# Log sums of a gated scan as two float32r products of a split operand, with a new table of priorities

## The chip, the cores and the metric

The kernel runs on one core of a Trainium2 chip. The metric is the device time of one execution in microseconds (us), as the median of several runs. A profile is one further execution, recorded by the hardware profiler.

## The reference

A complex gated linear attention (4 batches, 8 heads, 768 steps, head size 48) is followed by a token mixer of low rank and a channel mixer with a hidden size of 1536.

```python
mag = np.sqrt(a_re * a_re + a_im * a_im)
scale = np.minimum(mag, 0.999) / (mag + 1e-06)
a_re_n, a_im_n = (a_re * scale, a_im * scale)
for t in range(S):
    ar, ai = (a_re_n[:, :, t, :, None], a_im_n[:, :, t, :, None])
    new_re = ar * S_re - ai * S_im
    new_im = ar * S_im + ai * S_re
    kv = np.einsum('bhd,bhe->bhde', k[:, :, t], v[:, :, t])
    S_re, S_im = (new_re + kv, new_im)
    y[:, :, t] = np.einsum('bhd,bhde->bhe', q[:, :, t], S_re)
...
x = y.transpose(0, 2, 1, 3).reshape(B, S, H * D)      # (4, 768, 384)
h = x.transpose(0, 2, 1) @ U @ V                      # rank 32 over the tokens
u = x + h.transpose(0, 2, 1)
out = u + np.maximum(u @ w_ch1, 0.0) @ w_ch2
```

## The kernel before

**Chunks and groups.** The 4 x 768 tokens are cut into 24 chunks of 128 tokens (`i`, six to a batch), and the chunks into 12 groups of two (`g`). A gate is worked as a log magnitude and an angle, a group at a time. `gates(g)` returns four stages, recorded one after the other: `magnitudes` (L561), `totals` (L623), `turns` (L654) and `waves` (L698). Group 0 is worked chunk by chunk, all others in operations over 128 x 768 elements, two chunks of 384.

**The log sums.** `magnitudes_of` makes `l` (the tile `GL`, one buffer), which is minus the log of the clipped magnitude; the last step, an addition on VectorE, is L594 (L591 in group 0). For each of the two chunks `within` (L607) then has TensorE multiply `l` by two constant 128 x 128 matrices, `mid` and `fore`, which GpSimd makes at the start from a triangular matrix of zeros and ones, `prefix`, as differences of its columns; they hold -1, 0 and 1. The first product gives each token's log sum to the middle of its block of eight tokens (`es ps`), the second that from the block middles to the end of the half chunk (`ef ps`). Both are made in float32 at L611. ScalarE takes exponentials of them: `es` weighs q and k (`weigh`, L729), `ef` weighs k for the state (`onto_end`, L751). `of_blocks` (L637) makes 28 further sums of each column of `l` (`tot`, 16 small products a chunk, L647); they become the table `T` of decays between blocks. In the plan, `tot` comes behind the sums of its group through the name `("sums", g)`.

**The chunk.** `prep(i)` turns q and k by the angles and transposes them on TensorE (`tr`, L745) into the tile `QK`. `chain(i)` makes the products within blocks (`inner`, L784), scales `QK` between them on VectorE (`times`, L794, whose work the profile shows at L331), makes the `corners` (L830), the state's update (`dk`, L855) and the output (`y`, L886 and L894) into `xo`.

**The mixer.** `mixer(m)` works two chunks. When the six chunks of a batch are there, their rank-32 products (`mixed`, L928, copied to `r`) are made; then come a second `mixed` product per pair (L944), its addition to `xo` (L334), a transposition (`uTp`, L957), the products with w_ch1 (`up`, L969; in the last five mixers `few`, L1027) and those with w_ch2 (`down`, L1115 and L1158). The weights come in as pieces that ScalarE or VectorE and then three VectorE operations (L509 to L511) decode.

**The order.** The kernel doesn't issue its instructions where they stand in the source. Each operation is recorded by `PE`, `ACT`, `DVE`, `POOL` or `SP` (L303 to L316) with an engine, a cost, a rank, what it reads and what it writes. `Plan.order` (L80) then runs through time with these costs and gives each free engine the ready operation of the lowest priority value; this fixes one order for each engine, and the chip's engines work theirs strictly in that order. The priorities come from the table `URGENCY` (L26) by kind of work (`gates`, `angles`, `prep`, `levels`, `rest`, `w1`, `w2`) and number of the chunk or piece, and from `urgency` (L255) for the rest. As long as no mixer has begun and TensorE has nothing ready, the plan puts in a product of the identity with itself (`spare`, L1288), which nobody reads.

Of the kernel before, what the change touches and what calls it, by code (L numbers as in the profile page):

```python
# [9 lines left out]

FP = mybir.dt.float32
I32 = mybir.dt.int32
U32 = mybir.dt.uint32
AF = mybir.ActivationFunctionType
OP = mybir.AluOpType
PSUM = bass.MemoryType.PSUM

CH = 128
# [4 lines left out]
GC = 2  # L23
BLK = 32

URGENCY = {  # L26
    "w1": {0: 68.6, 1: 298.27, 2: 3233.01, 3: -108.72, 4: -43.26, 5: 87.5, 6: 342.55},
    "w2": {0: 1285.36, 2: 1292.54, 4: -1719.29, 6: -645.54, 8: 615.72, 10: -28.39, 12: 295.27},
    "gates": {0: -839.53, 1: -629.56, 2: -1280.45, 4: -490.35, 6: -36.77, 8: 432.19, 10: 283.33, 12: 174.0,
        14: -427.91, 16: -1044.12, 18: 390.39, 20: 16.15, 22: 442.09},  # L30
    "angles": {0: 244.5, 1: 803.69, 2: -1267.4, 4: -662.84, 6: 346.13, 8: -381.86, 10: -1492.55, 12: 857.33,
        14: 238.92, 16: -1275.26, 18: 27.58, 20: -452.39, 22: 700.28},
    "prep": {0: 403.21, 1: -1122.66, 2: -716.65, 3: -727.95, 4: -1687.67, 5: -1146.33, 6: -1196.73, 7: 372.34,
        8: -1231.6, 9: -737.98, 10: -968.71, 11: -301.11, 12: -1415.74, 13: -596.98, 14: 796.35, 15: -1516.54,
        16: 396.83, 17: 113.38, 18: 726.77, 19: -2850.56, 20: 477.2, 21: -682.71, 22: -1187.86, 23: -124.41},
    "levels": {0: -753.29, 1: -1075.23, 2: -3433.49, 3: -627.65, 4: -1402.65, 5: -2863.57, 6: 632.01, 7: 254.71,
        8: 403.03, 9: 467.1, 10: 379.45, 11: -2734.42, 12: -967.09, 13: 651.03, 14: -1988.63, 15: -5.33,
        16: -1244.43, 17: -678.34, 18: -1272.19, 19: 439.17, 20: -494.89, 21: -1132.39, 22: 188.76, 23: -7.55},
    "rest": {0: 430.24, 1: -1218.14, 2: -304.77, 3: -320.19, 4: 73.38, 5: 237.11, 6: 799.33, 7: 863.71, 8: 367.2,
        9: -579.61, 10: -1264.07, 11: -364.98, 12: -1258.34, 13: -1713.0, 14: -1491.2, 15: -35.56, 16: -1243.36,  # L40
        17: 71.85, 18: 200.85, 19: -580.61, 20: 849.69, 21: 576.05, 22: -124.73, 23: -299.46},
}


# [144 lines left out]
def kernel(  # L189
# [24 lines left out]
    nc = tc.nc  # L214
# [3 lines left out]
    DM = H * D  # L218
# [20 lines left out]
    NG = len(GROUPS)  # L239

    PAIRED = 5

    EARLY, SPREAD = 3, (0,)

    TA, TC, TQ, TK, TF, TH, NTOT = 0, 8, 12, 16, 18, 26, 28
    NP = 128 // R
# [7 lines left out]
    singles = pool("singles")  # L254
# [20 lines left out]
    def ring(base, tag, tiles):  # L275

        plan.buffer(base, tag, len(tiles))
        n = plan.turn[base] % len(tiles)
        makers[base] = lambda: tiles[n]

    def get(*base):
        if base not in T:
            T[base] = makers[base]()
        return T[base]
# [8 lines left out]
    def c_dve(n):  # L293
        return 0.15 + 0.00104 * n

    def c_one(n):
        return 0.15 + 0.00052 * n
# [5 lines left out]
    def PE(*a, **kw):  # L303
        plan.add("PE", *a, late=0.17, **kw)
# [4 lines left out]
    def DVE(cost, *a, **kw):  # L309
        plan.add("DVE", cost - 0.09, *a, late=0.09, **kw)  # L310
# [9 lines left out]
    def table(cost, rank, f, reads=(), writes=()):  # L320

        ACT(cost, rank, f, reads=list(reads) + [TABLE], writes=writes)
# [4 lines left out]
    def act(o, i, f, **kw):  # L327
        return nc.scalar.activation(out=o, in_=i, func=f, **kw)  # L328
# [21 lines left out]

    prefix = singles.tile([128, CH], FP, name="prefix")
    mask = singles.tile([128, 6, BLK], I32, name="mask")
    mid = singles.tile([128, CH], FP, name="mid")
    fore = singles.tile([128, CH], FP, name="fore")
    total = singles.tile([128, NTOT], FP, name="total")
    nc.gpsimd.memset(total, 0.0)
    F = singles.tile([128, GC, DM], FP, name="F")
    w1 = singles.tile([128, KD, FF], FP, name="w1")
    w2 = singles.tile([128, KF, DM], FP, name="w2")
# [26 lines left out]
    make_identity(nc, ident)  # L386

    GL = [singles.tile([128, GC * DM], FP, name="GL")]

    tail = ident[:, 127:128].to_broadcast([128, CH])  # L390
    AT, DG, VP = [], [], []
# [86 lines left out]
    def single(p, rank, to, o, pieces):  # L478
# [17 lines left out]
        x = lambda: get("cx", p)[:, 0:n]  # L496
        b, word = o.bitcast(U32), lambda a: a.bitcast(I32)
        one, two = c_one(n), c_dve(n)
# [45 lines left out]
    def gates(g):  # L544


        x, y, l, n, ar, ai = [(nm, g) for nm in ("x", "y", "l", "n", "ar", "ai")]
        z = y
        first = GROUPS[g][0]
        on_dve = g in SPREAD  # L550

        def of(b, i):
            return get(*b)[:, (i - first) * DM:(i - first + 1) * DM]
# [12 lines left out]
        def magnitudes_of(lo, hi):  # L566
            t, R1, W = t_of(lo, hi), ("gates", lo), (hi - lo) * DM
            ca, cd = c_act(W), c_dve(W)
            X, L, N = (b + (lo,) for b in (x, l, n))
            Y = [y + (i,) for i in range(lo, hi)]  # L570
            AR, AI = ([b + (i,) for i in range(lo, hi)] for b in (ar, ai))
            ACT(ca, R1, lambda: act(t(x), t(ar), AF.Square), AR, [X])
            ACT(ca, R1, lambda: act(t(y), t(ai), AF.Square), AI, Y)
            DVE(cd, R1, lambda: add(t(x), t(x), t(y)), Y, [X])
            DVE(c_one(W), R1, lambda: nc.vector.tensor_scalar(out=t(x), in0=t(x), scalar1=M2LO, scalar2=M2HI, op0=OP.max,
                                                              op1=OP.min), [], [X])
            if on_dve:
                DVE(c_one(W), R1, lambda: nc.vector.tensor_scalar(out=t(n).bitcast(U32), in0=t(ar).bitcast(U32), scalar1=0x7FFFFFFF, scalar2=None,
                                                                  op0=OP.bitwise_and), AR, [N])
            else:  # L580
                ACT(ca, R1, lambda: act(t(n), t(ar), AF.Abs), AR, [N])
            table(ca, R1, lambda: act(t(l), t(x), AF.Ln), [X], [L])
            table(ca, R1, lambda: act(t(x), t(l), AF.Exp, scale=0.5), [L], [X])
            DVE(cd, R1, lambda: add(t(x), t(x), t(n)), [N], [X])
            table(ca + 0.09, R1, lambda: act(t(y), t(l), AF.Exp, scale=-0.5, bias=leps), [L], Y)
            table(ca, R1, lambda: act(t(y), t(y), AF.Ln, bias=1.0), [], Y)

            if on_dve:
                DVE(c_one(W), R1, lambda: nc.vector.tensor_scalar(out=t(l), in0=t(l), scalar1=-0.5, scalar2=-LNMAX, op0=OP.mult,
                                                                  op1=OP.max), [], [L])  # L590
                DVE(cd, R1, lambda: add(t(l), t(l), t(y)), Y, [L])  # L591
            else:
                ACT(ca + 0.09, R1, lambda: act(t(l), t(l), AF.Relu, scale=-0.5, bias=lmax), [], [L])
                DVE(cd, R1, lambda: nc.vector.scalar_tensor_tensor(out=t(l), in0=t(l), scalar=LNMAX, in1=t(y), op0=OP.subtract,  # L594
                                                                   op1=OP.add), Y, [L])
            table(ca, R1, lambda: act(t(x), t(x), AF.Ln), [], [X])
            table(ca, R1, lambda: act(t(x), t(x), AF.Exp, scale=-1.0), [], [X])
            DVE(cd, R1, lambda: mul(t(x), t(x), t(ai)), AI, [X])
            if on_dve:
                DVE(c_one(W), R1, lambda: nc.vector.tensor_scalar(out=t(n), in0=t(ar), scalar1=0.0, scalar2=0.5, op0=OP.is_ge,  # L600
                                                                  op1=OP.subtract), AR, [N])
            else:
                ACT(ca + 0.09, R1, lambda: act(t(n), t(ar), AF.Sign, bias=tiny), AR, [N])
            for i in range(lo, hi):
                within(i, R1, L)

        def within(i, R1, L):  # L607
            ps, es = ("es ps", i), ("es", i)

            def summed(m, name, to, keeps):  # L610
                PE(0.65, R1, lambda: nc.tensor.matmul(out=get(*to), lhsT=m, rhs=of(l, i), start=True, stop=True),  # L611
                   [L, name], [to, ("sums", g, i)], takes=[keeps], steps=2)
            psum(ps, "T", [128, DM], [128, 512])
            buffer(es, "es", 3, [128, 2, DM])
            summed(mid, ("mid", 0), ps, es)
            for u in range(2):
                table(c_act(DM), R1, lambda u=u: act(get(*es)[:, u], get(*ps), AF.Exp, scale=1.0 - 2 * u), [ps], [es + (u,)])
            pf, ef = ("ef ps", i), ("ef", i)
            psum(pf, "T", [128, DM], [128, 512])
            summed(fore, ("fore", 0), pf, ef)  # L620
            table(c_act(DM), R1, lambda: act(get(*ef), get(*pf), AF.Exp, scale=-1.0), [pf], [ef])
# [722 lines left out]
```

## Time and profile before

| | |
|---|---|
| median of 3 runs | 688.33 us (687.19 to 691.46) |
| the profiled execution: its own time | 688.27 us |
| its span, first to last instruction | 686.5 us |
| granted TensorE clock, mean | 0.997 |
| TensorE products busy | 664.0 us (97%) |
| VectorE busy | 495.9 us (72%) |
| ScalarE busy | 413.8 us (60%) |

In the lines of the profile PE is a product on TensorE, PEld the load of its weights, DVE is VectorE, ACT is ScalarE, POOL is GpSimd and SP the engine that issues most transfers. A line of a group gives the source line, the engine, the operation, output<-inputs, the shapes and the count, then the busy time and the mean duration in ns, then the engine's idle time just before and what ended it. A product's duration holds its way through the array, so that products overlap; what one costs is seen from the distance of their starts, as the chain in order of time gives it (start, duration, what). A "pass" is one product instruction in the profile.

### The profile page before, as it was taken

The page shows a single profiled execution, that of the slowest core. Times are in us where ns is not written, and L with a number is a line of the kernel's source. Part 1 is how long each engine was busy: PE and PEld are TensorE (multiplying, and loading weights), DVE is VectorE, ACT ScalarE, POOL GpSimd, SP SyncE. Part 2 cuts the span into 40 slices and gives each one's busy share as a digit, 9 for nine tenths or more (in the row PEclk, how much of TensorE's full clock was granted, in tenths as well). Part 3 has the DMA queues.
Part 4 walks back from the last instruction along what each step waited for, and adds up shares of the span by engine and source line. Part 5 has one row for each costly group of instructions (what it writes and reads, how often), then busy time and mean ns, then how long its engine had stood idle before and what let it go on. Part 6 is the DMA issues. An engine that isn't in the chain of part 4 may idle for free.

```text
span 686.5 us, 26452 instructions
## 1 busy us (share of the span) xinstructions
PE 664.0 (97%) x11854; PEld 576.5 (84%) x11854; DVE 495.9 (72%) x882; ACT 413.8 (60%) x791; POOL 40.9 (6%) x81
## 2 busy tenths in 40 slices
PE   8999998999999999999999999999999989999998
PEld 7877776776888888788888888798899988999998
DVE  6798999657878867657685785396996855564734
ACT  6699999687596875937847767457435215031230
POOL 6000000001000000010010000000010000000000
PEclk9999999999999999999999999999999999999999
DMA  7756455461242330610514242112201001000000
GB/s 193 192 96 158 91 126 96 142 183 45 45 94 58 87 68 10 119 43 11 118 44 77 49 89 44 33 49 40 59 23 33 7 21 18 24 1 24 7 18 24
DMA packets 163329, 45.64 MB, mean 66 GB/s; under 512 B 158416, under 2 KB 160016, under 8 KB 163216
## 3 DMA queue, kind: packets, MB, share of 16 engines
q1 hardware_dynamic: 161008, 39.60, 26.7%
q0 software_dynamic: 2208, 4.35, 1.8%
q8 instruction: 93, 1.52, 0.9%
q14 instruction: 20, 0.16, 0.1%
HBM read 33.59 MB, written 4.72 MB: 56 GB/s over the span
## 4 chain that ended last, share of the span: by engine, by line
PE 78%; DVE 8%; ACT 6%; issue 2%; DVEq 0%; ACTq 0%
PE down L1158 18%; PE up L969 15%; PE few L1027 10%; PE inner L784 6%; PE tr L745 4%; PE dk L855 3%; PE y L894 3%; PE es ps L611 2%; PE down L1115 2%; PE ph L689 2%; PE ef ps L611 2%; PE spare L1288 2%; ACT gate L328 2%; PE y L886 2%; PE tot L647 1%
## 5 line engine op out<-in xcount | busy, mean ns | idle before, releaser
L969 PE MATMUL up<-uT,w 128*128 128x256 f32 x504 | 116.1, 382 | 0.0
L969 PEld LDWEIGHTS up<-uT,w 128*128 128x128 f32 x504 | 94.0, 190 | 15.2 <-DVE uT L959 0.3
L331 DVE TENSOR_TENSOR QK<-QK,T 112x512 f32<-112x512 f32 (+1 forms) x144 | 99.8, 715 | 7.4 <-PE corners L830 4.7
L748 ACT COPY QK<-tr 112x512 f32<-112x512 f32 x96 | 52.4, 586 | 43.3 <-PE tr L745 43.0
L328 ACT ACTIVATE gate<-gate 128x768 f32<-128x768 f32 (+1 forms) x89 | 69.3, 793 | 9.7 <-PE ph L689 6.8
L1158 PE MATMUL down<-w,h 128*128 128x192 f32 x396 | 73.5, 330 | 1.2 <-ACT gate L328 1.2
L1158 PEld LDWEIGHTS down<-w,h 128*128 128x128 f32 x396 | 64.1, 190 | 4.7 <-ACT gate L328 1.5
L1035 ACT COPY h<-few 128x512 f32<-128x512 f32 x30 | 17.4, 584 | 70.6 <-PE few L1027 62.5
L784 PEld LDWEIGHTS inner<-QK 112*32 112x32 f32 x4608 | 45.1, 109 | 17.3 <-issue 13.1
L745 PE MATMUL tr<-ident,QKC 128*112 128x128 f32 x384 | 52.9, 276 | 3.8 <-ACT QK L748 2.0
L334 DVE TENSOR_TENSOR h<-few,h 128x512 f32<-128x512 f32 x45 | 31.1, 692 | 34.3 <-PE few L1027 30.4
L784 PE MATMUL inner<-QK 112*32 112x16 f32 (+1 forms) x4608 | 50.7, 190 | 4.2 <-issue 3.9
L331 DVE TENSOR_TENSOR QKC<-qk,cs 128x768 f32<-128x768 f32 x48 | 45.0, 953 | 9.2 <-issue 3.4
L745 PEld LDWEIGHTS tr<-ident,QKC 128*112 128x112 f32 x384 | 42.2, 134 | 10.5 <-ACT QK L748 3.3
L1288 PE MATMUL spare<-ident 128*128 128x128 f32 x336 | 48.2, 291 | 1.9 <-POOL ident masks.py:199 1.4
L1288 PEld LDWEIGHTS spare<-ident 128*128 128x128 f32 x336 | 43.5, 201 | 5.7 <-issue 1.5
L334 DVE TENSOR_TENSOR xo<-down,xo 128x192 f32<-128x192 f32 (+1 forms) x79 | 29.7, 386 | 23.7 <-PE down L1158 23.5
L328 ACT ACTIVATE h<-up 128x512 f32<-128x512 f32 x42 | 24.9, 592 | 33.2 <-PE up L969 33.0
L1158 PE MATMUL down<-stage 128*128 128x192 f32 x198 | 36.8, 327 | 0.7 <-issue 0.7
L1027 PE MATMUL few<-gate,w 128*128 128x128 f32 x280 | 37.2, 282 | 0.0
L903 ACT COPY xo<-y 64x192 f32<-64x192 f32 x96 | 30.0, 313 | 8.7 <-PE y L894 7.0
L790 DVE COPY_PREDICATED DG<-mask,inner 128x128 f32<-128x128 int32 (+1 forms) x72 | 24.5, 343 | 14.6 <-PE inner L784 14.5
(137 smaller groups left out, 1217.7 us busy)
## 6 DMA issues: line engine op xcount, KB each, us to landing
stage<-in_moe_w_ch_dram SPq DMA_DIRECT2D x12, 768.0 KB, 5.2
gate<-in_a_re_dram SPq DMA_DIRECT2D x24, 192.0 KB, 3.5
gate<-in_a_im_dram SPq DMA_DIRECT2D x24, 192.0 KB, 4.0
qk<-in_q_dram SPq DMA_DIRECT2D x24, 192.0 KB, 2.9
qk<-in_k_dram SPq DMA_DIRECT2D x24, 192.0 KB, 3.4
VP<-in_v_dram SPq DMA_DIRECT2D x24, 192.0 KB, 3.7
AT<-DG SPq DMA_DIRECT2D x96, 32.0 KB, 2.0
out_dram<-xo POOLq DMA_DIRECT2D x12, 192.0 KB, 2.3
```

The source lines that it names most:

```text
L328: return nc.scalar.activation(out=o, in_=i, func=f, **kw)
L331: nc.vector.tensor_tensor(out=o, in0=a, in1=b, op=OP.mult)
L334: nc.vector.tensor_tensor(out=o, in0=a, in1=b, op=OP.add)
L611: PE(0.65, R1, lambda: nc.tensor.matmul(out=get(*to), lhsT=m, rhs=of(l, i), start=True, stop=True), [L, name], [to, ("sums", g, i)], takes ...
L745: nc.tensor.transpose(out=get(*ps)[0:DQ, j], in_=get(*qkc)[:, hh * HH + j].rearrange("p u d -> p (u d)")[:, 0:DQ], identity=ident)
L748: ACT(c_act(HH * CH) - 0.05, R1, lambda u=u, hh=hh, ps=ps: nc.scalar.copy(out=get(*QK)[:, u, hh * HH:(hh + 1) * HH], in_=get(*ps)[0:DQ]), ...
L784: nc.tensor.matmul(out=get(*ps)[js, h], lhsT=k_of(h)[:, js], rhs=part(q_of(h)[:, js], "p"), start=True, stop=True, tile_position=(0, j * BLK))
L903: ACT(c_act(HH * D) - 0.06, RR, lambda r=r, u=u: nc.scalar.copy(out=get(*xi).rearrange("p (a u d) -> p a u d", u=2, d=D)[r * HC:(r + 1) * ...
L969: nc.tensor.matmul(out=get(*ps)[:, e], lhsT=w1[:, f, (ff + e) * 128:(ff + e + 1) * 128], rhs=get(*uT)[:, f], start=(f == 0), stop=(f == KD ...
L1027: nc.tensor.matmul(out=get(*ps)[:, q], lhsT=w()[:, q * 128:(q + 1) * 128], rhs=v[0](), start=(n == 0 and q == 0), stop=True, skip_group_ch ...
L1158: nc.tensor.matmul(out=get(*to)[:, part], lhsT=x(j), rhs=y[:, j], start=(first and j == 0), stop=(j == KH - 1), skip_group_check=not first)
L1288: nc.tensor.matmul(out=spare[0], lhsT=ident, rhs=ident, start=True, stop=True)
```

## The change

From the fourth group on (`SPLIT = range(3, NG)`), `l` is no longer multiplied in float32. VectorE first copies it into a tile of type float32r (`gs0`), which rounds it, and then subtracts the copy from `l` into a second such tile (`gs1`). Each log sum is two float32r products, of `mid` or `fore` with `gs0` and with `gs1`, added up in the same accumulator. `mid` and `fore` become float32r tiles; the first three groups read them as float32 and multiply as before. `tot` still reads `l` itself; in the split groups it now stands behind the subtraction in the plan and no longer behind the sums. The two new tiles have one buffer each. The plan's cost of a sum is another one, and every value of the table of priorities is replaced, so that the order of the instructions changes on every engine.

```diff
+FR = mybir.dt.float32r
...
 URGENCY = {
-    "w1": {0: 68.6, 1: 298.27, 2: 3233.01, 3: -108.72, 4: -43.26, 5: 87.5, 6: 342.55},
+    "w1": {0: 507.18, 1: 192.13, 2: 2073.66, 3: 611.69, 4: 462.8, 5: 853.79, 6: -908.88},
...
+    SPLIT = range(3, NG)
...
-    mid = singles.tile([128, CH], FP, name="mid")
-    fore = singles.tile([128, CH], FP, name="fore")
+    mid = singles.tile([128, CH], FR, name="mid")
+    fore = singles.tile([128, CH], FR, name="fore")
...
+    GS = [[singles.tile([128, GC * DM], FR, name="GS%d" % n)] for n in range(2)]
...
+            if g in SPLIT:
+                for u in range(2):
+                    ring(("gs%d" % u, g), "gs%d" % u, GS[u])
+                a, b = ("gs0", g), ("gs1", g)
+                DVE(c_one(W), R1, lambda: nc.vector.tensor_copy(out=get(*a), in_=t(l)), [L], [a])
+                DVE(cd, R1, lambda: nc.vector.tensor_tensor(out=get(*b), in0=t(l), in1=get(*a).bitcast(FP), op=OP.subtract), [L, a], [b, ("sums", g, first)])
...
             def summed(m, name, to, keeps):
-                PE(0.65, R1, lambda: nc.tensor.matmul(out=get(*to), lhsT=m, rhs=of(l, i), start=True, stop=True),
-                   [L, name], [to, ("sums", g, i)], takes=[keeps], steps=2)
+
+                def both():
+                    for u in range(2):
+                        nc.tensor.matmul(out=get(*to), lhsT=m, rhs=of(("gs%d" % u, g), i), start=(u == 0), stop=(u == 1))
+                if g in SPLIT:
+                    PE(0.34, R1, both, [("gs0", g), ("gs1", g), name], [to], takes=[keeps], steps=2)
+                else:
+                    PE(0.65, R1, lambda: nc.tensor.matmul(out=get(*to), lhsT=m.bitcast(FP), rhs=of(l, i), start=True, stop=True),
+                       [L, name], [to, ("sums", g, i)], takes=[keeps], steps=2)
```

More of the change, by code (lines that the diff above doesn't have):

```diff
@@ L26 @@
 URGENCY = {
-    "w1": {0: 68.6, 1: 298.27, 2: 3233.01, 3: -108.72, 4: -43.26, 5: 87.5, 6: 342.55},
[L28 to L38, printed above, removed]
@@ L39 @@
-    "rest": {0: 430.24, 1: -1218.14, 2: -304.77, 3: -320.19, 4: 73.38, 5: 237.11, 6: 799.33, 7: 863.71, 8: 367.2,
-        9: -579.61, 10: -1264.07, 11: -364.98, 12: -1258.34, 13: -1713.0, 14: -1491.2, 15: -35.56, 16: -1243.36,
-        17: 71.85, 18: 200.85, 19: -580.61, 20: 849.69, 21: 576.05, 22: -124.73, 23: -299.46},
+    "w1": {0: 507.18, 1: 192.13, 2: 2073.66, 3: 611.69, 4: 462.8, 5: 853.79, 6: -908.88},
+    "w2": {0: 189.43, 2: 114.21, 4: -1320.06, 6: -411.01, 8: -1526.04, 10: -1090.37, 12: 82.17},
@@ new lines @@
+    "gates": {0: -827.04, 1: -108.62, 2: -696.89, 4: -39.79, 6: -687.19, 8: -2607.13, 10: 371.36, 12: -24.22,
+        14: 774.7, 16: 531.7, 18: 321.48, 20: -1678.42, 22: 980.05},
+    "angles": {0: -1147.31, 1: 406.08, 2: -964.97, 4: -1330.52, 6: -153.86, 8: -1139.52, 10: -1473.35,
+        12: -1198.81, 14: 295.29, 16: -775.57, 18: -1560.45, 20: 1004.56, 22: -3389.56},
+    "prep": {0: -219.88, 1: -695.76, 2: -491.16, 3: -128.4, 4: -1629.48, 5: -3199.56, 6: -3122.71, 7: -1308.34,
+        8: -221.61, 9: 103.41, 10: 122.86, 11: -724.56, 12: 450.24, 13: -2541.32, 14: 524.95, 15: -1332.44,
+        16: -1339.0, 17: -1104.55, 18: -705.05, 19: 639.2, 20: -1540.65, 21: -174.14, 22: 883.15, 23: 73.18},
@@ new lines @@
+    "levels": {0: 423.38, 1: -603.5, 2: -665.56, 3: -804.44, 4: -2754.53, 5: -876.32, 6: -1294.43, 7: -850.95,
+        8: -909.06, 9: 422.34, 10: -1475.51, 11: -838.81, 12: -1636.42, 13: -1137.32, 14: -702.51, 15: -3157.6,
+        16: 310.18, 17: 588.14, 18: -2846.07, 19: 998.8, 20: -970.35, 21: -2554.42, 22: 387.14, 23: 245.87},
+    "rest": {0: 744.4, 1: -649.7, 2: -487.33, 3: -1159.18, 4: -271.38, 5: -1480.58, 6: 613.49, 7: 627.13,
+        8: -870.05, 9: 586.56, 10: -622.69, 11: -79.63, 12: -1397.62, 13: 580.65, 14: 453.36, 15: -593.38,
+        16: 613.24, 17: 394.71, 18: -1216.42, 19: 88.32, 20: 52.34, 21: -3082.37, 22: -871.47, 23: -1242.83},
```

## The prediction

> **What bounds the kernel now.** I read the page's table of engines and the summary of the chain that ended last first, then the busy time in four stretches, then the chain in order of time where the log sums stand, then the groups of the operations that come and go.
>
> ```profile
> span 686.5 us, 26452 instructions
> PE 664.0 (97%) x11854; PEld 576.5 (84%) x11854; DVE 495.9 (72%) x882; ACT 413.8 (60%) x791; POOL 40.9 (6%) x81
> ...
> PE 78%; DVE 8%; ACT 6%; issue 2%; DVEq 0%; ACTq 0%
> ```
>
> TensorE is busy for 97% of the span and carries 78% of the chain. That is an average, so the stretches come next (columns: PE, weight loads, VectorE, ScalarE, GpSimd, then clock and DMA).
>
> ```profile
> 0.00:125.00 125.00, 113.26 (x2668) 94.00 (x2669) 108.59 (x185) 108.56 (x207) 11.28 (x35) 1.00 0.59 135
> 125.00:500.00 375.00, 370.92 (x6931) 310.37 (x6933) 271.29 (x455) 253.21 (x479) 20.82 (x32) 1.00 0.31 68
> 500.00:580.00 80.00, 76.74 (x1520) 72.67 (x1508) 58.32 (x116) 29.45 (x69) 3.90 (x7) 0.98 0.10 22
> 580.00:686.50 106.50, 103.11 (x763) 99.44 (x762) 57.71 (x127) 22.54 (x38) 4.88 (x9) 1.00 0.05 16
> ```
>
> There are two regimes. Up to about 125 us VectorE and ScalarE are each busy 87% of the time, and TensorE is partly filled with spare products:
>
> ```profile
> L1288 PE MATMUL spare<-ident 128*128 128x128 f32 x336 | 48.2, 291 | 1.9 <-POOL ident masks.py:199 1.4 <-issue 0.5
> ...
> 125.04 2.07 PE mixed L928 x24
> ...
> 130.57 0.22 PE spare L1288 x2
> 130.79 0.79 PE ph L689 x2
> 131.58 3.45 PE up L969 x16
> ```
>
> All 48.2 us of spares lie before the first `up` product at 131.58 us. From there real work fills TensorE: from 125 us on it is idle for 4.1 + 3.3 + 3.4 = 10.7 us out of 561.5, while VectorE has 104 us of idle time between 125 and 500 us. So TensorE work taken out after 131.58 us shortens the end nearly one for one, and VectorE work put in there is mostly hidden; before it, the reverse holds.
>
> **What the removed products cost.** Here is the chain in order of time (start, duration, passes) at two log sums, and at products of other widths:
>
> ```profile
> 144.53 0.65 PE es ps L611 x2
> 145.18 0.65 PE ef ps L611 x2
> 145.82 2.59 PE up L969 x12
> ...
> 450.97 4.88 PE down L1158 x30
> ...
> 597.70 13.55 PE few L1027 x120
> ```
>
> A float32 product stands as two passes. From 144.53 to 145.82 us lie four passes of 384 columns: 0.3225 us each, 0.645 us a sum. The other rows give 2.59/12 = 0.216 us for 256 columns, 4.88/30 = 0.163 for 192 and 13.55/120 = 0.113 for 128. Time goes with the columns, 0.84 to 0.88 ns each, and a pass with its own 128x128 weights can be as short as 0.113 us.
>
> Groups 3 to 11 hold 18 chunks with two sums each: 36 float32 products go, 72 float32r products come. In the order of the changed program, as in the old one, the four sums of group 3 come before the first `up` and those of the eight later groups behind it. So 32 sums count in full, and 4 fall in the early regime.
>
> No row shows a float32r product. Bounds for a sum made of two: if each is one pass as short as the shortest full-weight pass, 2 x 0.113 = 0.226 us, saving 0.419 a sum or 13.4 us over 32; if each is one pass at the float32 rate, 0.645 us and nothing saved; if each takes two passes as float32 does, 1.29 us and 20.6 us lost. I take one pass at half the time per column, which is what a 192-column pass takes: 0.163 us each, 0.326 a sum. Reason: I read the two passes of a float32 product as its operands being worked in parts, and the split hands over operands already cut into parts (the sums' other operand holds only -1, 0 and 1), so a quarter of the partial products is left. This saves 0.319 a sum, 10.2 us over 32, and 1.3 us over the early four. A weight load per product, as before with each pass, stays covered: 0.163 is longer than 0.113.
>
> The row that bears on this is 0.3225 us a pass and two passes a product. The Trainium skill, "FP8 and Floating Point Precision", section "TensorE Precision Notes", says that true FP32 needs four passes (high and low part of each operand against each other) and that reduced-precision FP32 is read as four bytes and cut to a shorter format. By its four against one a float32r product would be an estimated 0.645/4 = 0.161 us, 10.3 us saved over the 32 sums; the trace agrees with the page only so far as that it shows float32 as more than one pass, and no float32r row tests the rest.
>
> **What VectorE gets.** Per split group a copy of 128x768 and a subtraction of 128x768. The nearest rows are a one-source and a two-source operation of that size:
>
> ```profile
> L575 DVE TENSOR_SCALAR gate<-gate 128x768 f32<-128x768 f32 x11 | 6.1, 555 | 0.1
> L594 DVE SCALAR_TENSOR_TENSOR GL<-GL,gate 128x768 f32<-128x768 f32 x11 | 10.5, 955 | 2.9 <-ACT GL L328 2.9
> ```
>
> That is 0.555 + 0.955 = 1.51 us a group, 13.6 us for nine. If the rounding copy loses the fast rate it costs 0.955 like the two-source row, 3.6 us more in all. Eight groups put 12.1 us (at most 15.3) into a stretch where VectorE has 104 us idle: I cost them at nothing on the path. If that cover failed, the whole 12.1 us would come back.
>
> The sums now wait for the split and not for `GL`, and stand in TensorE's queue ahead of `tot`, `up` and `down` products. Before, they already stood close behind `GL`:
>
> ```profile
> PE es ps L611 <- DVE GL L594: 0.7, 1, 0.7
> ...
> 189.57 0.95 DVE L594 SCALAR_TENSOR_TENSOR GL<-GL,gate 128x768 f32<-128x768 f32 x1
> 190.43 0.30 DVE L790 COPY_PREDICATED DG<-mask,inner 128x128 f32<-128x128 int32 x1
> 192.17 0.81 PE L611 MATMUL es ps<-GL,mid 128*128 128x384 f32 x2
> ```
>
> In this group `GL` ends at 190.52 and the sum starts at 192.17: 1.65 us, just over the 1.51 that the split needs. In the changed order four of the nine splits have one or two other VectorE instructions between copy, subtraction and their input, but the sums have been moved as well, so that `up` or `down` passes lie before most of them. I take no net wait, and keep a bound of one split (1.5 us) for each of the eight groups.
>
> **The new priorities.** Up to the first `up`, TensorE's queue holds the same products in both orders, but 178 spares instead of 168. At 0.22 us each (the row at 130.57) this is +2.2 us, against -1.3 us from the four sums: +0.9 us if TensorE's own queue sets the start. VectorE gets five operations more ahead of the first `mixed` addition: one split (1.51 us) and one weight piece that used to follow:
>
> ```profile
> L511 DVE SCALAR_TENSOR_TENSOR w<-stage,w 128x768 uint32<-128x768 uint32 x12 | 11.5, 955 | 0.2
> L334 DVE CUSTOM_DVE_ANT_0 w<-w,stage 128x1536 uint16<-128x1536 uint16 x12 | 11.4, 953 | 0.5 <-ACT stage L328 0.5
> L509 DVE TENSOR_SCALAR w<-w 128x768 uint32<-128x768 uint32 x12 | 6.7, 555 | 7.3 <-ACT w L328 7.2
> ```
>
> That is 0.955 + 0.953 + 0.555 = 2.46 us, 3.97 with the split, +4.0 us if VectorE sets the start throughout. VectorE waits just there in the old trace:
>
> ```profile
> 128.86 1.02 DVE L334 TENSOR_TENSOR xo<-mixed,xo 128x384 f32<-128x384 f32 x2 [4.85 <-PE mixed L944]
> ```
>
> so part of the 4.0 falls into that wait. I take +2 us between 0.9 and 4.0. The last 810 TensorE and 189 VectorE instructions stand in the same order as before: the end after the last attention chunk, with its 3.4 us of idle time, should be a shifted copy. For the middle I assume that the idle time stays as it was, and allow 4 us either way, about half of the 4.1 + 3.3 us idle between 125 and 580 us.
>
> **The sum.** The profiled execution took 688.27 us, 1.8 more than its span; the median is 688.33, so nothing has to be converted. 688.3 - 10.2 + 2 = 680.1, and I say 680.
>
> **The rivals.**
> - The start eats the gain. If the first `up` comes the whole 4.0 us late and the middle gains 4 us of idle time, 688.3 - 10.2 + 4 + 4 = 686. For it: VectorE at 87% before 125 us. Against: the 4.85 us wait.
> - No faster pass. If float32r streams at the float32 rate, 688.3 + 2 = 690. For it: every row of TensorE lies at 0.84 ns a column or above. Against: all those rows are float32.
> - VectorE is late, and the kernel slower. TensorE waits in each of the eight groups for the split behind its interposed work (1 us: 1.51 plus two operations of 0.55, less the 1.65 of slack), and the 1.51 us is handed on to the `QK` products queued behind it on VectorE, for which `inner` products wait: 2.5 us a group, 20 us, 688.3 - 10.2 + 2 + 20 = 700. It decides from (10.2 - 2)/8 = 1.0 us a group. For it: the small slack. Against: TensorE has waited for `GL` only once, 0.7 us, and VectorE has 13 us idle per group.
> - Two passes for each float32r product: 688.3 + 20.6 + 2 = 711. Nothing speaks for it but that two passes are all the trace shows.
>
> **How the numbers follow.** Chances: the forecast 0.65, with its own range 674 to 685; the start eats the gain 0.11; no faster pass 0.07; VectorE late 0.12; two passes 0.05. About 1% (below 681.4 or above 695.2) can be told from no change here, the three runs spanning 0.6%. Of the forecast's 0.65, 0.54 lies below 681.4 and 0.11 between it and 685. Faster 0.54; within 1% 0.11 + 0.11 + 0.07 = 0.29; slower 0.12 + 0.05 = 0.17. The range runs from 673 (a pass near the 0.113 bound with the start on time, or 4 us of idle time gained) to 693, which takes in the first two rivals and leaves out the slow ones.
>
> **What would show it.** Right: `es ps<-GS` and `ef ps<-GS` in 72 single passes about 0.163 us apart; first `up` at 132 to 136 us; TensorE idle from there about 10 us; `GS` copies of 0.555 us; VectorE busy near 509 us. Wrong: passes at 0.32 us or 144 of them; waits of PE on `GS` above 1 us in most groups; a first `up` beyond 136 us; a new wait of `inner` on VectorE's `QK`.

## The result and the profile after

The changed kernel took 681.14 us (median of 4 runs, 679.66 to 681.81), the kernel before 688.88 beside it: a ratio of 0.9882 with an interval of 0.9846 to 0.9917, so 1.2% faster. Three more comparisons gave 0.9913 (0.9892 to 0.9934), 0.9880 (0.9855 to 0.9905) and 0.9880 (0.9856 to 0.9904). One run of the kernel before in the last of these sets took 817.84 us at a granted clock of 0.753; its median in the table below, 690.77, counts that run, the ratios don't. The forecast was 680. The profiled execution took 680.91 us with a span of 679.1.

The head, the engines and the chain's engines on the page of the changed kernel (its lines stand some 2 to 16 lower in the source: the log sums are L623, float32 ones L627, `up` L985, `down` L1174, `ph` L705, `inner` L800; in the experiments' kernels a few lines off again):

```profile
span 679.1 us, 26495 instructions
PE 655.3 (96%) x11874; PEld 576.1 (85%) x11874; DVE 507.0 (75%) x900; ACT 411.7 (61%) x791; POOL 40.6 (6%) x81
...
PE 70%; DVE 11%; ACT 11%; issue 3%; DMA 3%; POOL 1%; SPq 0%; DVEq 0%; ACTq 0%; POOLq 0%
```

TensorE has 20 passes more, two for each of the 10 more spares, and is busy 8.7 us less; VectorE is busy 11.1 us more. By stretches:

```profile
0.00:125.00 125.00, 111.16 (x2670) 93.37 (x2670) 109.97 (x188) 107.13 (x203) 10.69 (x34) 1.00 0.59 137
125.00:500.00 375.00, 369.62 (x6974) 315.56 (x6972) 285.10 (x479) 256.61 (x491) 22.20 (x33) 1.00 0.32 67
500.00:580.00 80.00, 78.77 (x1558) 73.21 (x1547) 59.85 (x120) 26.60 (x63) 2.81 (x6) 1.00 0.10 22
580.00:679.10 99.10, 95.76 (x704) 93.95 (x702) 52.09 (x116) 21.41 (x36) 4.85 (x9) 1.00 0.05 17
```

The log sums in the chain in order of time, against the four passes of 0.3225 us shown before:

```profile
146.61 2.59 PE up L985 x12
149.20 0.35 PE es ps L623 x2
149.55 0.34 PE ef ps L623 x2
149.89 2.16 PE up L985 x10
```

Four float32r passes take 0.69 us where four float32 passes took 1.29: 0.173 us a pass. The new operations, from the view of the tile `GS` (minimum, median and maximum in ns, first and last start in us):

```profile
L603 DVE CAST GS<-GL x9: 551/559/561, 109.3 to 460.3; 128x768 fp32r<-128x768 f32 x9
L604 DVE TENSOR_TENSOR GS<-GL,GS x9: 949/957/960, 110.3 to 460.9; 128x768 fp32r<-128x768 f32 x9
```

And the start of the mixers in the changed kernel's timeline:

```profile
127.88 1.56 ACT L330 ACTIVATE gate<-gate 128x768 f32<-128x768 f32 x2
128.05 0.95 POOL L699 DMA_DIRECT2D gate<-F  x1 [115.68 <-DVE F L711]
129.34 0.46 ACT L947 COPY r<-mixed 128x384 f32<-128x384 f32 x1
132.19 1.11 DVE L975 COPY uT<-uTp 128x384 f32<-128x384 f32 x2 [0.17 <-PE uTp L973]
134.45 0.88 PE L705 MATMUL ph<-gate,prefix 128*128 128x384 f32 x2 [1.30 <-DMA gate<-F]
135.17 2.11 PE L985 MATMUL up<-uT,w 128*128 128x256 f32 x9
```

The same work in the timeline of the kernel before:

```profile
124.65 0.95 POOL L683 DMA_DIRECT2D gate<-F  x1 [112.46 <-PE y L894]
127.18 0.48 ACT L931 COPY r<-mixed 128x384 f32<-128x384 f32 x1 [1.59 <-PE mixed L928]
130.06 1.11 DVE L959 COPY uT<-uTp 128x384 f32<-128x384 f32 x2 [0.18 <-PE uTp L957]
```

The first `up` comes at 135.17 us, 3.8 later than before (131.42 in the timeline; the chain of before counts it from 131.58). Its operand `uT` is there at 133.30, 2.1 us later than before (131.17). The rest is `ph`, which stands ahead of `up` in TensorE's queue and waits for GpSimd's transfer. That was issued only at 128.05, and it is on the chain for 6.27 us, where the transfer issued at 124.65 before took 3.86 us to land:

```profile
128.05 6.27 DMA gate<-F
134.32 0.14 issue
134.45 0.88 PE ph L705 x2
```

Why it took longer, the trace doesn't show.

The table gives for each kernel what was read in its trace, in us: the start of the first `up`, the time in the 64 passes (32 in two kernels) of the log sums behind it, each block counted from the end of the pass before it (less some 0.18 us for its way through the array) to the start of the next other pass, and the stretch from the first `up` to the end of the last `y`. After that come 107.47 to 107.49 us in every kernel.

| kernel | median (runs) | ratio to before | first up | sums | first up to last y |
|---|---|---|---|---|---|
| before | 688.39, 688.99, 690.77 (three sets) | 1 | 131.4 | 23.2 | 447.6 |
| changed, first | 681.14 (4) | 0.9882 | 135.2 | 13.7 | 436.5 |
| changed, again | 682.39 (6) | 0.9913 | 135.0 | 13.7 | 438.7 |
| changed, third | 681.18 (6) | 0.9880 | 135.7 | 13.7 | 436.2 |
| changed, fourth | 681.94 (6) | 0.9880 | 136.8 | 13.7 | 437.0 |
| new order, float32 rate | 689.11 (12) | 1.0013 | 136.4 | 22.8 | 443.7 |
| new order, no split | 689.12 (12) | 1.0004 | 135.0 | 22.8 | 446.7 |
| old order, split | 685.52 (12) | 0.9961 | 133.0 | 16.9 | 444.0 |
| one product | 682.16 (6) | 0.9918 | 139.5 | 9.1 | 435.8 |
| one product, again | 680.54 (6) | 0.9881 | 134.8 | 9.1 | 436.3 |
| short second product | 680.27 (5) | 0.9859 | 135.6 | 10.5 | 435.4 |
| three moves at the start | 686.92 (12) | 0.9976 | 133.5 | 14.3 | 442.0 |
| 15 spares fewer | 689.69 (12) | 0.9998 | 142.7 | 13.8 | 440.0 |

Between the two first profiles the account closes: +3.8 at the start, -9.5 in the sums, -1.6 in the rest of the middle, 0 at the end, together -7.4 with the rounding, the difference of the spans. Medians and profiles can differ: the profiled execution of the kernel with 15 spares fewer (691.96 us) lies 2.3 us above its median, that of the three moves (684.76 us) 2.2 us below.

### The profile page after: what moved, and what is told of

It is laid out like the page before. It is cut to its first block, busy times and chain, and to the rows that moved or that the text cites. A ratio compares the mean times of both kernels' runs of the same rounds, so it can differ in the third digit from the quotient of the medians.

```text
span 679.1 us, 26495 instructions
## 1 busy us (share of the span) xinstructions
PE 655.3 (96%) x11874; PEld 576.1 (85%) x11874; DVE 507.0 (75%) x900; ACT 411.7 (61%) x791; POOL 40.6 (6%) x81
## 4 chain that ended last, share of the span: by engine, by line
PE 70%; DVE 11%; ACT 11%; issue 3%; DMA 3%; POOL 1%; SPq 0%; DVEq 0%; ACTq 0%; POOLq 0%
PE down L1174 19%; PE up L985 14%; PE few L1043 10%; PE inner L800 5%; PE tr L761 4%; PE dk L871 3%; PE y L910 2%; ACT gate L330 2%; ACT L327 2%; PE ph L705 2%; ACT QK L764 2%; DVE QK L333 2%; PE y L902 2%; PE spare L1304 1%; ACT xo L919 1%
## 5 line engine op out<-in xcount | busy, mean ns | idle before, releaser
L985 PE MATMUL up<-uT,w 128*128 128x256 f32 x504 | 116.3, 382 | 0.6 <-issue 0.6
L985 PEld LDWEIGHTS up<-uT,w 128*128 128x128 f32 x504 | 93.5, 190 | 13.6 <-issue 1.1
L1174 PE MATMUL down<-w,h 128*128 128x192 f32 x396 | 73.3, 330 | 0.0
L1174 PEld LDWEIGHTS down<-w,h 128*128 128x128 f32 x396 | 64.0, 190 | 3.1 <-issue 1.6
L800 PEld LDWEIGHTS inner<-QK 112*32 112x32 f32 x4608 | 45.2, 109 | 19.0 <-issue 14.1
L800 PE MATMUL inner<-QK 112*32 112x16 f32 (+1 forms) x4608 | 50.7, 190 | 4.6 <-issue 3.3
L1304 PE MATMUL spare<-ident 128*128 128x128 f32 x356 | 50.1, 286 | 2.2 <-POOL ident masks.py:199 1.4
L1304 PEld LDWEIGHTS spare<-ident 128*128 128x128 f32 x356 | 45.2, 197 | 5.9 <-issue 1.7
L1174 PE MATMUL down<-stage 128*128 128x192 f32 x198 | 36.5, 327 | 0.0
L1118 POOL DMA_DIRECT2D out_dram<-xo x32 | 18.4, 574 | 296.5 <-DVE xo L336 282.7
L330 ACT ACTIVATE h<-h 128x512 f32<-128x512 f32 x30 | 18.9, 630 | 26.3 <-DVE h L336 26.1
```

The costliest lines, as they stand in the source:

```text
L800: nc.tensor.matmul(out=get(*ps)[js, h], lhsT=k_of(h)[:, js], rhs=part(q_of(h)[:, js], "p"), start=True, stop=True, tile_position=(0, j * BLK))
L985: nc.tensor.matmul(out=get(*ps)[:, e], lhsT=w1[:, f, (ff + e) * 128:(ff + e + 1) * 128], rhs=get(*uT)[:, f], start=(f == 0), stop=(f == KD ...
L1118: queue.dma_start(out=out[b, c * CH:(c + 1) * CH, lo:hi], in_=get("xo", i)[:, lo:hi])
L1174: nc.tensor.matmul(out=get(*to)[:, part], lhsT=x(j), rhs=y[:, j], start=(first and j == 0), stop=(j == KH - 1), skip_group_check=not first)
L1304: nc.tensor.matmul(out=spare[0], lhsT=ident, rhs=ident, start=True, stop=True)
```

## The experiments

My theory was that TensorE sets the time from the first `up` on and VectorE's split is hidden. The rivals were that the new order made the gain, and that VectorE or another engine takes the bound over.

**The changed kernel as base.** No edit; it ran beside each set of the others.

> The changed kernel once more, as the base for the runs beside it. Both theories: 680 to 682 us, first up near 135 us, a ratio to before of 0.985 to 0.992.

682.39 us, a little above that, with a ratio of 0.9913 and the first `up` at 135.0. The two later bases came out at 681.18 and 681.94.

**Float32 rate in the new order.** Same recorded operations and order, same number of passes.

```diff
-    for u in range(2):
-        nc.tensor.matmul(out=get(*to), lhsT=m, rhs=of(("gs%d" % u, g), i), ...)
+    nc.tensor.matmul(out=get(*to), lhsT=m.bitcast(FP), rhs=of(("gs0", g), i).bitcast(FP), ...)
```

> The changed kernel in its own order, VectorE's split included, but every split sum is one float32 product of the rounded part (the remainder is left out, so the sums are rounded): two passes of 0.323 us in place of two of 0.173. Theory (TensorE sets the time from the first up on): 32 sums x 0.30 = 9.6 us more than the changed kernel, about 691, and so some 2 us above the kernel before, because the new order starts the mixers 3.8 us later. Rival (the new order made the gain): 681 to 684.

689.11 us, a ratio of 1.0013 (0.9988 to 1.0038), 6.7 us above the changed kernel beside it. The chain shows the passes at their old length:

```profile
146.90 0.65 PE es ps L622 x2
147.55 0.65 PE ef ps L622 x2
148.19 2.59 PE up L984 x12
```

So the new order without the faster pass gives nothing, and the rival falls. But 9.1 us more in the sums became 6.7 us in the time: not quite one for one. The profile of the base beside it holds a wait of 2.3 us ahead of pass 9619 in which TensorE waits for nothing that the profile shows (more on these waits below), and this kernel's profile doesn't. Against the first and the third profile of the changed kernel, which don't hold it either, the stretch from the first `up` to the last `y` is 7.2 and 7.5 us longer.

**The new order with no split.** Float32 sums from `GL`, VectorE's two operations left out.

```diff
-  nc.vector.tensor_copy(out=get(*a), in_=t(l))
-  nc.vector.tensor_tensor(out=get(*b), in0=t(l), in1=get(*a).bitcast(FP), op=OP.subtract)
-  rhs=of(("gs0", g), i).bitcast(FP)
+  rhs=of(l, i)
```

> The changed kernel's order with float32 sums read from GL in all groups, and VectorE's copy and subtraction left out: the new order alone. Theory (VectorE's 1.5 us a group is hidden behind the first up and costs at most its one split before it): 0 to 1.5 us less than the kernel with float32-rate sums and the split kept, which took 689.1, so 687.6 to 689.1. Rival (the split costs time in the middle too): 686 or less.

689.12 us, 1.0004 (0.9976 to 1.0033): the same, within these intervals of some 2 us, as with VectorE's 13.6 us of split. The traces of the two kernels have the same passes in the same order and can be laid side by side: from the first `up` to behind the last sum the split costs 0.5 us (behind that, this profile holds the wait ahead of pass 9619 again, 2.3 us). So in the new order the split is hidden but for 0.5 us of the middle.

**The old order with the split.** The kernel before, with the split in the same recorded operation as the last step of the log.

```diff
+    if g in SPLIT:
+        nc.vector.tensor_copy(out=GS[0], in_=t(l))
+        nc.vector.tensor_tensor(out=GS[1], in0=t(l), in1=GS[0].bitcast(FP), op=OP.subtract)
...
+    for u in range(2):
+        nc.tensor.matmul(out=get(*to), lhsT=m, rhs=GS[u][...], start=(u == 0), stop=(u == 1))
```

> The kernel before in its old order and priorities, with the split put straight behind the last step of the log in groups 3 to 11 and float32r products in the places of the float32 ones. Theory: 9.6 us less on TensorE, given back where the sum stood closer behind GL than the 1.5 us of the split: by the starts in the old trace 1.1 + 0.4 + 0.5 us in three of the eight groups and 1.2 us in the early one, so 688.9 - 9.6 + 3.2 = 682.5. Rival (the new order made the gain): 688 or more. Rival (VectorE late): about 690 to 695, with TensorE waiting for the remainder in most groups.

685.52 us, 0.9961 (0.9942 to 0.9980): 2.9 us gained, less than my 6.4 and more than either rival gave. Of the 9.5 us that the passes save, 3.2 come back as waits inside the sums (16.9 against 13.7 us), and the first `up` comes 1.6 us later than in the kernel before. From the view of the tile `es ps`, two of the rows that say what was waited for in the whole run ahead of the first of the two sums of a chunk (total us, times; weight loads and passes are both counted):

```profile
  DVE GS L602: 3.1, 6
  ACT es L330: 2.6, 5
```

So the sums wait for the split, and also for ScalarE's exponentials `es` of the sum before. The largest loss outside the sums behind the first `up`, 1.1 us, is another product that waits for VectorE behind the split:

```profile
321.79 0.56 DVE L601 CAST GS<-GL 128x768 fp32r<-128x768 f32 x1
322.38 0.96 DVE L602 TENSOR_TENSOR GS<-GL,GS 128x768 fp32r<-128x768 f32 x1
323.26 0.48 DVE L803 COPY_PREDICATED DG<-mask,inner 128x128 f32<-128x128 int32 x2
323.69 0.75 PE L843 MATMUL corners<-QK 112*32 112x32 f32 x64 [1.04 <-DVE DG L803]
```

That is the kind of loss that I had given to the slower rival, though at `corners`, for `DG`. The waits of `inner` for `QK` that I had named hardly change: behind the first `up` their weight loads wait once, 0.3 us, before and here.

So new order and split need each other: the pass is worth 2.9 us in the old order and 6.7 to 7.9 in the new one (against the two kernels with float32 sums, each with the base beside it).

**Only the product with the rounded part.** The product with the remainder is left out.

```diff
-    for u in range(2):
-        nc.tensor.matmul(..., rhs=of(("gs%d" % u, g), i), start=(u == 0), stop=(u == 1))
+    nc.tensor.matmul(..., rhs=of(("gs0", g), i), start=True, stop=True)
```

> The changed kernel in its own order, each split sum only the product with the rounded part (the product with the remainder is left out; VectorE still makes both parts). Theory: 32 x 0.173 = 5.5 us less than the changed kernel, about 675.6. Rival (another engine has become the bound behind the first up): 679 to 681.

682.16 us against 682.39 beside it: nothing gained, though the sums took 4.6 us less. In this profile the first `up` was 4.4 us late behind an early stretch at half the clock (12.5 to 19.3 us after the start in the trace; the times in the expectation that follows are too early), so it ran once more.

> The kernel with only the product with the rounded part in each split sum, once more (its first profile had the clock at one half from 6.8 to 13.7 us after the start, and the first up 4.3 us later than in the changed kernel). If that was chance: first up near 135 us and 677 to 679 us in total, 3 to 5 us less than the changed kernel. If 36 fewer passes shift the places where TensorE waits for its instructions to worse ones: first up near 135 us, 2 to 3 us more of such waits, and a total within 2 us of the changed kernel.

680.54 us against 681.18: 0.6 us, well within the noise. The first `up` is at 134.8, the sums take 4.5 us less, and yet the stretch from the first `up` to the last `y` is 436.3 as in the base. The chain shows one place where the gain went, and the base's timeline the same work:

```profile
496.07 1.24 PE inner L799 x82
497.31 0.69 PE down L1173 x3
498.00 2.09 issue
500.09 1.95 PE down L1173 x11
```

```profile
499.29 1.26 PE L800 MATMUL inner<-QK 112*32 112x16 f32 x128
500.48 1.24 PE L1174 MATMUL down<-stage,more 128*128 128x192 f32 x6
```

In the base the six `down` passes follow each other; with one product TensorE stands 2.09 us in the middle of them and nothing in the profile is waited for ("issue"). Counted through the trace, waits of this kind stand ahead of passes 5172, 7969, 9619 and 10765, which are 92 to 97 above a multiple of 127, in all 5.2 us; the base has 1.6 us behind the first `up`, ahead of 5045, 5172 and 10637 (92, 92 and 96). Laid side by side pass by pass, this kernel loses 1.0, 1.2, 2.3 and 1.4 us on the base at its four places and gains 2.3 us where the base waits. I had expected 2 to 3 us more of such waits; it is 3.6. A transfer on the instruction queue (16,384 bytes) ends 1.2 to 1.7 us before each such wait ends, at 498.81 us before the one shown. The trace of the base has 93 such transfers for 11,874 passes, 127.7 passes each. I read this as TensorE running ahead of its own instructions, in blocks of 127 passes: with 36 passes fewer the ends of the blocks fall on other work, behind runs of short passes, where a block is used up too fast. That the places are fixed by the count of passes is shown; that short passes are what makes a place bad is not.

**A short second product.** To keep the number of passes, the second product stays but is cut to 32 x 16; the rest of the remainder is left out.

```diff
+    nc.tensor.matmul(out=get(*to)[0:32, 0:16], lhsT=m[:, 0:32], rhs=of(("gs1", g), i)[:, 0:16], start=False, stop=True, ...)
```

> The changed kernel with the product with the remainder cut to 32 rows by 16 columns in each split sum (the rest of the remainder is left out): as many passes as before, so that TensorE's waits for instructions fall on the same places, but less time in them. Theory (TensorE time comes through where those places stay): 2 to 4.5 us less in the sums, waits for instructions as in the changed kernel, so 677.5 to 680. Rival (another engine takes the gain): 681 to 683.

680.27 us against 681.94, just outside what I expected (0.9859, 0.9836 to 0.9882, against 0.9880, so the two intervals overlap). The sums took 3.2 us less and the middle 0.8 to 1.6 less than in the last two bases. The two larger waits for instructions stood two and five passes ahead of the base's (5043 and 10632), and they were longer: 1.17 and 1.55 us in place of 0.39 and 0.88 in the third base. So part of the saved time came back there. Why is open: no log sum stands in the 127 passes ahead of either place.

**Fifteen spares fewer.** Every seventh of 105 spares ahead of the first `up` is left out.

```diff
+    spares = [j for j, n in enumerate(line) if n == -1]
+    for j in reversed(spares[60:165:7]):
+        del line[j]
```

> The changed kernel with 15 of its 178 spares left out before the first up product, so that every later pass has a number lower by 30. Theory (TensorE waits for instructions after every 127 passes, and the order was laid out for these places): first up the same or up to 1 us earlier, about 2 us more of such waits behind it, a total 1 to 2 us above the changed kernel although TensorE does less. Rival (the number of passes doesn't matter): the same total or less.

689.69 us (0.9998, 0.9973 to 1.0023): 7.8 us slower than the base for leaving out products that nobody reads. I had expected 1 to 2, all of it behind the first `up`. Behind it 3.0 to 3.8 us came, among them waits of 2.2 and 1.5 us ahead of passes 9619 and 10765. The larger part came before: the first `up` stood at 142.7, 7.0 us later than in the third base. Of this, 1.4 us aren't from the edit: this profile has a stretch at half the clock from 12.7 to 16.1 us, ahead of the first spare that is left out. The chain there, and the stretch from 85 to 100 us in this kernel and then in the third base:

```profile
86.54 0.52 PE inner L800 x42
87.06 1.96 issue
...
91.22 0.96 PE dk L871 x41
92.19 2.61 issue
```

```profile
85.00:100.00 15.00, 10.44 (x256) 8.01 (x252) 8.63 (x15) 9.05 (x18) 0.00 (x0) 0.89 0.36 73
```

```profile
85.00:100.00 15.00, 13.93 (x290) 11.16 (x286) 14.21 (x23) 13.67 (x30) 0.00 (x0) 1.00 0.58 128
```

TensorE waits for instructions for 4.6 us, the granted clock falls to 0.89 in the same stretch, and VectorE and ScalarE, which set the pace there, are busy 8.6 and 9.1 us in place of 14.2 and 13.7. How much is the moved block ends and how much the clock, these runs don't tell apart.

**Three moves at the start**, to win back the late first `up`.

```diff
+    line.remove(at_ph[7]); line.insert(line.index(at_up[0, 0]) + 1, at_ph[7])
+    line.remove(at_r[0]); line.insert(line.index(at_mixed[0]) + 1, at_r[0])
+    # and four spares ahead of the second mixed product taken out
```

> The changed kernel with three moves around the first mixer, everything else in its order: the angle product of chunk 7, which waits for a GpSimd transfer, goes behind the first six up products; ScalarE copies r before it goes on with the next gates; four spares ahead of the second mixed product are left out. Theory (a late start is handed on one for one): the first up comes at about 132.5 to 133 us in place of 135.1, the 0.65 us of the angle product still has to be done, so 1.5 to 2.1 us less than the changed kernel in the total. Rival (work freed at the start is waited for later): the first up comes early and the total stays within 0.5 us.

686.92 us (0.9976, 0.9949 to 1.0004): the first `up` came at 133.5, 2.2 us earlier than in the base, and the total was 5.7 us worse. The lead was gone after 10 us. Two rows of its timeline:

```profile
137.12 0.84 ACT L331 ACTIVATE gate<-gate 128x768 f32<-128x768 f32 x1 [5.26 <-PE ph L707]
...
141.31 5.45 PE L990 MATMUL up<-uT,w 128*128 128x256 f32 x24 [1.68 <-ACT h L331]
```

ScalarE's next gate waits for the moved `ph`, the copies of `up`'s results into `h` stand behind that gate, and TensorE waits for `h`: by the passes at 151 us this kernel is 1.1 us behind the base. So taking away the wait for the transfer in this way won nothing. Some 2.9 us more are lost about 557 us, at a wait for instructions of 1.8 us and a stretch at half clock: four spares fewer had moved the block ends by eight passes. The profile shows 3.5 us of the 5.7; and since the spares were changed together with the two moves, it isn't shown what the moves alone would do. No kernel here that makes the full sums was faster than the changed one.

## Why the prediction was right, and where it was wrong

- **The passes: right in mechanism, a little off in size.** 72 single passes, 0.173 us in place of 0.163. Over the 32 sums 9.5 us were saved where I had 10.2. The four-against-one count of the Trainium skill, "FP8 and Floating Point Precision", section "TensorE Precision Notes", comes near: a float32r product took 0.173 us, against 0.161 estimated by that count from the 0.645 us of a float32 product here, a ratio of 3.7. The trace shows the float32 product as two passes, not four.
- **The start: near the bound, and the wrong cause.** The first `up` came 3.8 us late (3.6, 4.3 and 5.4 in the other three profiles) where I took 2 between 0.9 and 4.0; in the fourth, at 136.8 us, it showed one of my signs of being wrong. I had named VectorE and TensorE's queue. The trace shows ScalarE, which copies `r` behind two gate operations, on the way to a `uT` that is 2.1 us late, and then GpSimd's transfer behind a later `F`, for which `ph` waits. The experiment with three moves won nothing by undoing this.
- **VectorE hidden: right, but by the new order.** With no split the new order takes the same time. In the old order, 3.2 us of waits inside the sums, 1.6 us at the first `up` and 1.1 us at `corners` came back. My check of the slack, 1.65 us against 1.51, described that order, not the changed one.
- **The middle unchanged, the end a shifted copy: about right.** The rest of the middle gained 1.6 us between the first profiles, within the 4 that I allowed (1.9 and 1.1 in the third and fourth profile of the changed kernel, 0.6 lost in the second, which holds the wait ahead of pass 9619); the end is equal to 0.02 us. Behind the first `up` the waits for instructions come to 3.3 us in the profile of before and to 1.7 in the first one of the changed kernel. The difference is as large as the gain; other waits changed too, so this isn't a full account.
- **"Nearly one for one" was wrong as a rule.** 9.1 us more in the sums gave 6.7; 4.5 us less with 36 passes fewer gave 0.6; 15 spares fewer cost 7.8. What I had taken for idle time that stays as it was is in part "issue": as I read it, TensorE waits for its own instructions, at places fixed by the count of passes. The kernel itself knows of them. `Plan` is made with `(95, 127, 16, 3.7)`, and by these numbers `taken` (L100) lets every 127th pass, counted from pass 95, begin no earlier than 3.7 us after the pass 143 places ahead of it began. So both orders were laid out with such waits in the plan, and an edit that changes the count of passes moves the places away from where the plan had them. The change keeps two passes to a sum. The forecast was near in part by luck: my sum came out because a saving over-sized by 0.7 us and a start under-sized by 1.8, both of which make the time longer, met 1.6 us of gain in the middle: 680.1 + 0.7 + 1.8 - 1.6 = 681.0, where the profiled execution took 680.91.
- **The rivals.** "No faster pass" and "two passes" are excluded by the passes. "The start eats the gain" was half true. "VectorE late" is in part what the split alone does in the old order, though the whole still came out 0.4% faster there. In the changed kernel the sums wait for `GS` once behind the first `up`, 0.3 us at a weight load.

## What to carry to other kernels

Before a saving on a saturated engine is booked, look at its waits for nothing ("issue"): if they repeat after a fixed number of instructions, look whether the change keeps that number, and try a kernel that does beside one that doesn't. An order made by hand or by a planner belongs to the operations that it was made for, so a new operation and a new order have to be tried together and apart. Filler work that nobody reads may still set where later waits fall, and whether a wait at the head of a queue is a loss isn't known until what stands behind it in the next engine's queue has been followed.

## What the runs showed of the hardware

- TensorE stood still for up to 2.6 us, with nothing in the profile to wait for, ahead of passes 90 to 98 above a multiple of 127, in the kernels counted and in the kernel before too (passes 9620 and 10766). The place goes with the count and not with the work: ahead of pass 10764, 10765 or 10766 stand waits of 1.0 to 2.1 us in five kernels, at `inner` in some and at `few` in others. The one in the chain of before:

```profile
558.17 1.15 PE inner L784 x81
559.32 2.08 issue
561.39 0.25 PE inner L784 x6
```

- Whether such a wait appears can differ between executions of one kernel: 2.3 us ahead of pass 9619 in the second profile of the changed kernel, none in the other three.
- The granted clock falls to one half for 3.4 us at a time, in some places close behind such waits: from 562.7 us in the profile of before, where the wait ahead of pass 10766 had taken 2.1 us and ended at 561.4, and from 94.6 us in the kernel with fewer spares, as the wait of 2.6 us ends. It doesn't follow every one: the wait of 2.3 us ahead of pass 9619 in the second profile of the changed kernel has no such stretch behind it, and the stretch from 12.7 us in the kernel with fewer spares stands behind none of these places.
- The rounding copy to float32r kept the fast rate of a one-source operation: 559 ns for 128x768 against 957 for the subtraction.
